# Attention scores of pooled keys: one product of 64 rows and 72 columns for each head in place of one of 128 rows and 144 columns for two

## The chip, the cores and the metric

The kernel runs on one core of a Trainium2 chip. The metric is the time of one execution on the device in microseconds (us); the median of three runs before is 1643.18 us (1641.29 to 1643.87).

## What is computed

Eight batches of eight heads, 576 queries, 576 keys and values of 64 numbers, all float32. Keys and values are first averaged over groups of 8, so each head has 72 pooled keys. Softmax attention over these 72 follows, and its output, 4608 rows of 512 numbers, goes through two two-layer networks.

```python
k_p = k.reshape(B, H, Sp, pool, D).mean(axis=3)      # B, H = 8, 8; Sp, pool, D = 72, 8, 64
v_p = v.reshape(B, H, Sp, pool, D).mean(axis=3)
scores = scale * np.matmul(q, k_p.transpose(0, 1, 3, 2))
scores = scores - np.max(scores, axis=-1, keepdims=True)
attn = np.exp(scores)
attn = attn / (np.sum(attn, axis=-1, keepdims=True) + 1e-09)
attn_out = np.matmul(attn, v_p)
...
h = x @ w_in;  x = np.maximum(0.01 * h, h) @ w_out   # first network, 512 -> 2048 -> 512
h = x @ w_in2; r = np.maximum(h, 0.0); out = (r * r) @ w_out2
```

## The kernel before

**Stages.** The attention is one generator, `attention()`. Its first batch is written out in order by hand (`first_batch`, L662); the other seven are advanced in pieces (`advance`, L1195) between the steps of the first network's first tiles, which TensorE works on in the same time (`first`, L851, and `second`, L881). All attention work is over at about 480 us. What follows, the rest of the first network and the whole second one, is products of 128 rows with 256 to 512 columns in TensorE's order, with none of the changed lines in it.

**The attention of a batch.** The 576 queries come in five chunks of 128, 128, 64, 128 and 128 tokens, named by their first token: 0, 128, 256, 320, 448. `prepare_k` (L422) pools the keys, transposes them (`trk`) and writes them into one of two tiles `kT` (L456 to L464); `prepare_v` does the values. For each chunk `stage_a` (L529) transposes the queries (`trq`), so that `qT[:, m]` holds the 64 numbers of head 2m on rows 0 to 63 and those of head 2m+1 on rows 64 to 127, for each of the `NP` = 4 pairs m. `stage_parts` (L545) makes the scores (L554), the negated maxima (L564), the exponentials (L571, or for the last three batches L576 and L580) and the normalised weights `p`; `keys_part` and `rest_part` (L599, L610) transpose these into `pt` and `pr`; `stage_d` (L629) multiplies with the values.

**The scores.** `kT` is a tile `[128, 4, 2, 72]`: of the 144 columns of a pair the first 72 hold the keys of head 2m on rows 0 to 63 with zeros below, the last 72 those of head 2m+1 on rows 64 to 127 with zeros above. The zeros are written once, at the start, by GpSimd (L347). So one product of all 128 rows, 144 columns wide, gives the scores of two heads side by side. Four such products make a chunk: two into the PSUM bank of score tile `s..._0` (heads 0 to 3), two into that of `s..._1` (heads 4 to 7). The queries are the weights that TensorE loads, 128 columns wide (64 in the 64-token chunk), and the keys stream.

**What sets the order.** The framework schedules the instructions of each engine from the code's order and its own costs when the kernel is built; each engine then runs its list strictly in that order, waiting where something isn't there. Score tiles come from a ring of four PSUM banks (`ps_w`; in the first batch `ps_a`), which the products `h` and `o` and the transposes use too.

Of the kernel before, what the change touches and what calls it, by code (L numbers as in the profile page):

```python
# [8 lines left out]
F32 = mybir.dt.float32  # L9
F32R = mybir.dt.float32r  # L10
U32 = mybir.dt.uint32
AF = mybir.ActivationFunctionType
ALU = mybir.AluOpType
# [4 lines left out]
P = 128  # L18
POOL = 8
KM = 64  # L20
# [7 lines left out]
def raw(ap):  # L28

    return ap.bitcast(F32)  # L30
# [3 lines left out]
def attention_two_mlps(  # L34
# [11 lines left out]
    nc = tc.nc  # L46
    B, H, S, D = q.shape
# [3 lines left out]
    SP = S // POOL  # L51
    KR = SP - KM
    NP = H // 2
# [82 lines left out]
    def work(name, n=TT, early=False):  # L136
        if early:
            return ps_a.tile([P, n], F32, tag="acc", name=name)
        return ps_w.tile([P, n], F32, tag="w", name=name)
# [182 lines left out]
    def attention():  # L322

        with ExitStack() as s:
# [4 lines left out]
            one = s.enter_context(tc.tile_pool(name="one", bufs=1, side="right"))  # L329
# [5 lines left out]
                out=mask, in_=mask, compare_op=ALU.is_ge, fill=0.0, base=0,  # L335
# [3 lines left out]
                out=mask, in_=mask, compare_op=ALU.is_ge, fill=0.0, base=KR - 1,  # L339
                pattern=[[KR, H], [0, D]], channel_multiplier=-1,  # L340
            )

            kT = [one.tile([P, NP, 2, SP], F32, name=f"kT{i}") for i in range(2)]
            vM = [one.tile([P, NP, 2, D], F32R, name=f"vM{j}") for j in range(2)]
            vR = one.tile([3 * RG, NP, 2 * D], F32R, name="vR")
            for i in range(2):
                nc.gpsimd.memset(kT[i], 0.0)  # L347
                nc.gpsimd.memset(raw(vM[i]), 0.0)
            pt_h = one.tile([P, NP, SPANS[0]], F32R, name="pt_h")
            pt_l = one.tile([P, NP, SPANS[0]], F32R, name="pt_l")  # L350
# [2 lines left out]
            def pooled(dst, src):  # L353

                for n in (POOL * D // 2, POOL * D // 4, D):
                    nc.vector.tensor_tensor(
                        out=dst if n == D else src[:, :, 0:n], in0=src[:, :, 0:n], in1=src[:, :, n:2 * n], op=ALU.add
                    )

            def pooled_pe(name, src):  # L360

                ps = work(name, NP * D).rearrange("p (m d) -> p m d", d=D)
                for m in range(0, NP, 2):
                    for j in range(POOL):
                        nc.tensor.matmul(
                            ps[:, m:m + 2], ident, src[m // 2][:, :, j * D:(j + 1) * D],
                            start=j == 0, stop=j == POOL - 1,
                        )
                    yield ps
# [52 lines left out]
            def prepare_k(b):  # L422
                kr, kk = KV.pop(("k", b))
                i = b % 2
                kd = ap1.tile([P, NP, D], F32, tag="kd", name=f"kd{b}")
                rr = ap1.tile([KR * H, 2, D], F32, tag="rr", name=f"rr{b}")
                pooled(rr[:, 0:1], kr)
                nc.vector.tensor_copy(rr[:, 1], rr[:, 0])
                if b in K_ON_PE:
                    for ps in pooled_pe(f"kp{b}", kk):  # L430
                        yield
                    nc.scalar.copy(kd, ps)
                else:
                    for m in range(0, NP, 2):
                        pooled(kd[:, m:m + 2], kk[m // 2])
                        if b > 0:
                            yield
                            continue
                        tr = work("trk0") if m == 0 else tr
                        nc.tensor.transpose(  # L440
                            tr[:, m * D:(m + 2) * D], kd[:, m:m + 2].rearrange("p a d -> p (a d)"), ident
                        )
                        yield
                if b > 0:
                    load_v(b)
                    tr = work(f"trk{b}")
                for g in range(2 if b > 0 else 0):
                    nc.tensor.transpose(
                        tr[:, g * P:(g + 1) * P], kd[:, 2 * g:2 * g + 2].rearrange("p a d -> p (a d)"), ident
                    )  # L450
                nc.tensor.transpose(
                    tr[:, 2 * P:2 * P + KR * H], rr.rearrange("p a d -> p (a d)"), ident[:KR * H, :KR * H]
                )
                for r in range(2):
                    rows = slice(r * D, (r + 1) * D)
                    nc.scalar.activation(  # L456
                        kT[i][rows, :, r, 0:KM], tr[rows, 0:2 * P].rearrange("p (m x) -> p m x", x=KM),
                        AF.Copy, scale=scale / POOL,
                    )
                    nc.scalar.activation(  # L460
                        kT[i][rows, :, r, KM:SP],
                        tr[rows, 2 * P:2 * P + KR * H].rearrange("p (m r x) -> p m r x", r=2, x=KR)[:, :, r],
                        AF.Copy, scale=scale / POOL,
                    )  # L464
                yield
# [48 lines left out]
            for b in range(B):  # L514
                at = 0
                for span in range(len(SPANS)):
                    off = 0
                    while off < SPANS[span]:
                        n = min(P, SPANS[span] - off)
# [21 lines left out]
            def stage_b(*chunk):  # L541
                for _ in stage_parts(*chunk):
                    pass

            def stage_parts(b, span, at, off, n):  # L545
                qT = qt.pop((b, at))
                x = xp.tile([P, H, SP], F32, tag="x", name=f"x{b}_{at}", bufs=2)
                sm, rs = (xp.tile([P, H, 1], F32, tag=g, name=f"{g}{b}_{at}") for g in ("sm", "rs"))
                scores = []
                for e in range(2):  # L550
                    sc = work(f"s{b}_{at}_{e}", early=b == 0)[:, :H // 2 * SP].rearrange("p (h x) -> p h x", x=SP)
                    scores.append(sc)
                    for m in range(2):
                        nc.tensor.matmul(  # L554
                            sc[:n, 2 * m:2 * m + 2].rearrange("p a x -> p (a x)"),
                            qT[:, 2 * e + m, :n],
                            kT[b % 2][:, 2 * e + m].rearrange("p a x -> p (a x)"),
                            start=True, stop=True,
                        )
                yield  # L560
                tops = []
                for e, sc in enumerate(scores):
                    mx = xp.tile([P, 4, 1], F32, tag="mx", name=f"mx{b}_{at}_{e}")
                    nc.vector.tensor_reduce(out=mx[:n], in_=sc[:n], axis=AX.X, op=ALU.max, negate=True)  # L564
                    tops.append(mx)
                yield
                for e, (sc, mx) in enumerate(zip(scores, tops)):
                    hs = slice(4 * e, 4 * e + 4)
                    if b < EARLY:
                        for h in range(4):  # L570
                            nc.scalar.activation(  # L571
                                x[:n, 4 * e + h], sc[:n, h], AF.Exp,
                                bias=mx[:n, h], accum_out=sm[:n, 4 * e + h],
                            )
                        continue
                    nc.vector.tensor_tensor(  # L576
                        out=x[:n, hs], in0=sc[:n], in1=mx[:n].to_broadcast([n, 4, SP]), op=ALU.add
                    )
                if b >= EARLY:
                    nc.scalar.activation(x[:n], x[:n], AF.Exp)  # L580
                    nc.vector.tensor_reduce(out=sm[:n], in_=x[:n], axis=AX.X, op=ALU.add)
                yield
                nc.vector.tensor_scalar(out=sm[:n], in0=sm[:n], scalar1=1e-9, scalar2=None, op0=ALU.add)
                nc.vector.reciprocal(rs[:n], sm[:n])
                pp = xp.tile([P, DM + 6 * RG], F32, tag="p", name=f"p{b}_{at}", bufs=2)
                nc.gpsimd.tensor_tensor(
                    out=pp[:n, 0:DM].rearrange("p (h x) -> p h x", x=KM), in0=x[:n, :, 0:KM],
                    in1=rs[:n].to_broadcast([n, H, KM]), op=ALU.mult,
                )
                for g in range(2):  # L590
                    hs = slice(4 * g, 4 * g + 4)
                    o = pp[:n, DM + 3 * g * RG:DM + 3 * (g + 1) * RG].rearrange("p (r h x) -> p r h x", r=3, x=KR)
                    nc.gpsimd.tensor_tensor(
                        out=o, in0=x[:n, hs, KM:].unsqueeze(1).to_broadcast([n, 3, 4, KR]),
                        in1=rs[:n, hs].unsqueeze(1).to_broadcast([n, 3, 4, KR]), op=ALU.mult,
                    )
                pr[b, at] = pp
# [199 lines left out]
            for i in range(nch + 1, len(chunks) + 1):  # L797
# [3 lines left out]
                if i < len(chunks):  # L801
                    b = chunks[i][0]
# [13 lines left out]

    ready, marks = [0], []
    att = attention()
    STORES, made = [], 0

# [485 lines left out]
```

## Time and profile before

| | |
|---|---|
| median of three runs | 1643.18 us |
| the profiled execution, its own time | 1641.07 us |
| its span, first to last instruction | 1639.3 us |
| TensorE (PE) busy | 1602.6 us, 98% |
| its weight loads (PEld) | 1466.8 us, 89% |
| VectorE (DVE) busy | 1388.1 us, 85% |
| ScalarE (ACT) busy | 1008.1 us, 61% |
| GpSimd (POOL) busy | 117.3 us, 7% |
| DMA queue of the data | 66.3% of 16 engines |
| mean granted clock of TensorE | 0.996 of 2.4 GHz |

Multiplies are recorded with the time in which their data passes the array and comes out; they overlap, so that the time one costs in a row of many is the distance between two starts, not the length of a record. Weight loads have records of their own (PEld) and lie beside the multiplies of the weights before. A float32 product that isn't a transpose is recorded as two multiplies with a load each; the kernel's products of 256 and more columns are in the one-multiply format (`F32R`). Of a form such as `128*64 128x144`, the first pair is rows and columns of the weights, the second what streams.

### The profile page before, as it was taken

To read this page: it belongs to the slowest core of one execution; us is meant where nothing else is said; L and a number is where in the kernel's file an instruction comes from. 1 tells how busy PE (TensorE), PEld (TensorE's weight loads), DVE (VectorE), ACT (ScalarE), POOL (GpSimd) and SP (SyncE) were. 2 spreads that over 40 slices of the span, in tenths; PEclk is the share of its full clock that TensorE was granted. 3 is DMA by queue.
4 is the path that set the end of the run, shared out by engine and by line. 5 is a ranking of instruction groups with operands and counts; after the bars stand their busy time and mean duration, and the time that the engine had idled before them with its cause. 6 is when DMAs were issued, how large, how long until landed. Compare 5 with 4: busy or idle time off the path is not lost.

```text
span 1639.3 us, 25990 instructions
## 1 busy us (share of the span) xinstructions
PE 1602.6 (98%) x9032; PEld 1466.8 (89%) x9032; DVE 1388.1 (85%) x2070; ACT 1008.1 (61%) x1930; POOL 117.3 (7%) x149
## 2 busy tenths in 40 slices
PE   5999999999999999999999999999999999999999
PEld 4877788888888999999999999998998998998997
DVE  6899776789889999979759589889789799799687
ACT  6777677755667867667557547456456455465454
POOL 4121222223110000000000000000000000000000
PEclk9999999999999999999999999999999999999999
DMA  8675554777547688887766764865865756756655
GB/s 212 190 203 169 144 134 139 233 217 224 180 157 257 244 284 296 265 304 231 225 190 204 236 186 151 281 196 149 275 187 176 254 177 198 241 171 209 196 167 167
DMA packets 223730, 340.94 MB, mean 208 GB/s; under 512 B 56176, under 2 KB 138096, under 8 KB 223600
## 3 DMA queue, kind: packets, MB, share of 16 engines
q1 hardware_dynamic: 223280, 338.76, 66.3%
q8 instruction: 72, 1.18, 0.3%
q10 hardware_dynamic: 320, 0.52, 0.1%
q14 instruction: 58, 0.48, 0.1%
HBM read 268.44 MB, written 69.21 MB: 206 GB/s over the span
## 4 chain that ended last, share of the span: by engine, by line
PE 83%; DVE 8%; ACT 4%; DMA 3%; issue 1%; SPq 0%; POOL 0%; ACTq 0%; DVEq 0%; POOLq 0%
PE psum L1078 14%; PE psum L317 14%; PE psum L319 14%; PE psum L318 14%; PE psum L1079 7%; PE h L317 3%; PE h L319 3%; PE h L318 3%; PE acc L318 3%; PE acc L319 2%; PE acc L317 2%; PE s L554 1%; ACT x L571 1%; DMA xs<-x 1%; DVE hl_out L245 1%
## 5 line engine op out<-in xcount | busy, mean ns | idle before, releaser
L1078 PE MATMUL psum<-wb_out,oh 128*128 128x512 f32 x1008 | 352.8, 394 | 0.0
L317 PE MATMUL psum<-xh,wb_in 128*128 128x384 f32 x1008 | 337.3, 335 | 2.2 <-ACT s L1052 1.2
L319 PE MATMUL psum<-xh,wb_in 128*128 128x384 f32 x1008 | 336.8, 334 | 0.0
L318 PE MATMUL psum<-xl,wb_in 128*128 128x384 f32 x1008 | 336.8, 334 | 0.0
L930 ACT CAST oh<-g 128x768 fp32r<-128x768 f32 x252 | 210.3, 836 | 160.1 <-PE psum L1078 89.3
L1079 PE MATMUL psum<-wb_out,ol 128*128 128x256 f32 x1008 | 281.8, 280 | 0.0
L931 DVE TENSOR_TENSOR ol<-g,oh 128x768 fp32r<-128x768 f32 x252 | 239.4, 954 | 17.4 <-ACT oh L930 14.9
L1078 PEld LDWEIGHTS psum<-wb_out,oh 128*128 128x128 f32 x1008 | 189.6, 188 | 43.1
L317 PEld LDWEIGHTS psum<-xh,wb_in 128*128 128x128 f32 x1008 | 189.2, 188 | 3.9 <-ACT s L1052 1.5
L318 PEld LDWEIGHTS psum<-xl,wb_in 128*128 128x128 f32 x1008 | 189.2, 188 | 0.2
L319 PEld LDWEIGHTS psum<-xh,wb_in 128*128 128x128 f32 x1008 | 189.2, 188 | 0.0
L1079 PEld LDWEIGHTS psum<-wb_out,ol 128*128 128x128 f32 x1008 | 188.8, 187 | 0.2
L984 ACT CAST wb_in<-wb_in 128x512 fp32r<-128x512 f32 x144 | 89.3, 621 | 146.4 <-DMA wb_in<-ws_in 141.4
L985 DVE TENSOR_TENSOR wb_in<-wb_in 128x512 fp32r<-128x512 f32 x144 | 98.7, 688 | 80.3 <-ACT wb_in L984 79.8
L934 DVE TENSOR_TENSOR g<-g,g 128x768 f32<-128x768 f32 x144 | 136.0, 952 | 1.5 <-ACT g L1006 1.0
L317 PE MATMUL h<-xh,hl_in 128*128 128x512 f32 (+1 forms) x320 | 121.8, 381 | 4.0 <-DVE pt_r L619 2.8
L317 PE MATMUL acc<-gh,hl_out 128*128 128x512 f32 (+1 forms) x320 | 120.2, 382 | 1.4 <-ACT hl_out L244 1.1
L318 PE MATMUL acc<-gl,hl_out 128*128 128x512 f32 (+1 forms) x320 | 118.6, 373 | 0.7 <-DVE gl L865 0.7
L319 PE MATMUL h<-xh,hl_in 128*128 128x512 f32 (+1 forms) x320 | 118.7, 371 | 0.0
L318 PE MATMUL h<-xl,hl_in 128*128 128x512 f32 (+1 forms) x320 | 118.1, 369 | 0.0
L319 PE MATMUL acc<-gh,hl_out 128*128 128x512 f32 (+1 forms) x320 | 117.9, 371 | 0.0
L318 PE MATMUL psum<-ol,wb_out 128*128 128x384 f32 x336 | 112.6, 335 | 0.0
(161 smaller groups left out, 3113.7 us busy)
## 6 DMA issues: line engine op xcount, KB each, us to landing
wb_in<-wd_in SPq DMA_DIRECT2D x108, 512.0 KB
wb_out<-wd_out SPq DMA_DIRECT2D x108, 512.0 KB
wb_in<-ws_in SPq DMA_DIRECT2D x144, 256.0 KB
wb_out<-ws_out SPq DMA_DIRECT2D x144, 256.0 KB
xs<-x SPq DMA_DIRECT2D x18, 768.0 KB
out_dram<-o SPq DMA_DIRECT2D x23, 384.0 KB
q<-in_q_dram SPq DMA_DIRECT2D x32, 256.0 KB
v<-in_v_dram SPq DMA_DIRECT2D x64, 128.0 KB
```

The lines of the kernel that those rows point to most:

```text
L245: nc.vector.tensor_tensor(out=lo, in0=w, in1=raw(hi), op=ALU.subtract)
L317: nc.tensor.matmul(outp, ah, bh, start=first, stop=False, **kw)
L318: nc.tensor.matmul(outp, ah, bl, start=False, stop=False, **kw)
L319: nc.tensor.matmul(outp, al, bh, start=False, stop=last, **kw)
L554: nc.tensor.matmul(sc[:n, 2 * m:2 * m + 2].rearrange("p a x -> p (a x)"), qT[:, 2 * e + m, :n], kT[b % 2][:, 2 * e + m].rearrange("p a x - ...
L930: nc.scalar.copy(hi, src)
L931: nc.vector.tensor_tensor(out=lo, in0=src, in1=raw(hi), op=ALU.subtract)
L934: nc.vector.tensor_tensor(out=out_, in0=a, in1=b, op=ALU.subtract)
L984: nc.scalar.copy(whole[:, 0], raw(whole[:, 1]))
L985: nc.vector.tensor_tensor(out=whole[:, 1], in0=raw(whole[:, 1]), in1=raw(whole[:, 0]), op=ALU.subtract)
L1078: nc.tensor.matmul(outp, ah, b, start=first, stop=False, skip_group_check=True)
L1079: nc.tensor.matmul(outp[:, 1], al, b[:, 0], start=False, stop=last, skip_group_check=True)
```

## The change

Each head gets a product of its own: the 64 rows of its queries and keys, 72 columns wide, 8 a chunk in place of 4. `kT` loses the dimension that held the zeros, and the two memsets of it go. The eight products alternate between the lower and the upper 64 rows, and the bank now goes by the half: the even heads (rows 0 to 63) go to score tile `s..._0`, the odd ones to `s..._1`. So the maxima, the exponentials and the sums of a tile are those of every other head, and L576 writes its result into every other block of 72 columns of `x`.

```diff
-            kT = [one.tile([P, NP, 2, SP], F32, name=f"kT{i}") for i in range(2)]
+            kT = [one.tile([P, NP, SP], F32, name=f"kT{i}") for i in range(2)]
...
-                nc.gpsimd.memset(kT[i], 0.0)
...
-                        kT[i][rows, :, r, 0:KM], tr[rows, 0:2 * P].rearrange("p (m x) -> p m x", x=KM),
+                        kT[i][rows, :, 0:KM], tr[rows, 0:2 * P].rearrange("p (m x) -> p m x", x=KM),
...
-                        kT[i][rows, :, r, KM:SP],
+                        kT[i][rows, :, KM:SP],
...
-                    for m in range(2):
-                        nc.tensor.matmul(
-                            sc[:n, 2 * m:2 * m + 2].rearrange("p a x -> p (a x)"),
-                            qT[:, 2 * e + m, :n],
-                            kT[b % 2][:, 2 * e + m].rearrange("p a x -> p (a x)"),
-                            start=True, stop=True,
-                        )
+                for m in range(NP):
+                    for r, sc in enumerate(scores):
+                        rows = slice(r * D, (r + 1) * D)
+                        nc.tensor.matmul(sc[:n, m], qT[rows, m, :n], kT[b % 2][rows, m], start=True, stop=True)
...
-                    hs = slice(4 * e, 4 * e + 4)
                     if b < EARLY:
-                        for h in range(4):
+                        for m in range(NP):
+                            h = 2 * m + e
                             nc.scalar.activation(
-                                x[:n, 4 * e + h], sc[:n, h], AF.Exp,
-                                bias=mx[:n, h], accum_out=sm[:n, 4 * e + h],
+                                x[:n, h], sc[:n, m], AF.Exp,
+                                bias=mx[:n, m], accum_out=sm[:n, h],
                             )
                         continue
                     nc.vector.tensor_tensor(
-                        out=x[:n, hs], in0=sc[:n], in1=mx[:n].to_broadcast([n, 4, SP]), op=ALU.add
+                        out=x[:n].rearrange("p (m r) x -> p r m x", r=2)[:, e], in0=sc[:n],
+                        in1=mx[:n].to_broadcast([n, NP, SP]), op=ALU.add,
                     )
```

The order that the framework makes of it differs on TensorE almost only in the score products. In the rows below `s_128_0` is the score tile 0 of chunk 128, `acc` and `h` are products of the first network, `trq` and `pt` transposes; the last pair of numbers is the output's shape. A typical group, chunk 128 of batch 2 on TensorE, stands before as

```order
L319 MATMUL acc_0_3_727<-gh_0_15_1753,hl_out_15_1760 128x512
L554 MATMUL s_128_0_1912<-kT_179,qT_128_1802 128x144 x2
L554 MATMUL s_128_1_1915<-kT_179,qT_128_1802 128x144 x2
L317 MATMUL h_1_1_1936<-xh_1_0_1831,hl_in_1_1866 128x512
L318 MATMUL h_1_1_1936<-xl_1_0_1832,hl_in_1_1866 128x512
```

and after the change (the score line is now L555) as

```order
L319 MATMUL acc_0_3_745<-gh_0_15_1791,hl_out_15_1798 128x512
L555 MATMUL s_128_0_1954<-kT_179,qT_128_1840 128x72
L555 MATMUL s_128_1_1955<-kT_179,qT_128_1840 128x72
L555 MATMUL s_128_0_1954<-kT_179,qT_128_1840 128x72
L555 MATMUL s_128_1_1955<-kT_179,qT_128_1840 128x72
L555 MATMUL s_128_0_1954<-kT_179,qT_128_1840 128x72
L555 MATMUL s_128_1_1955<-kT_179,qT_128_1840 128x72
L555 MATMUL s_128_0_1954<-kT_179,qT_128_1840 128x72
L555 MATMUL s_128_1_1955<-kT_179,qT_128_1840 128x72
L317 MATMUL h_1_1_1982<-xh_1_0_1873,hl_in_1_1908 128x512
```

Its neighbours, products of 128 rows, are the same; between them TensorE now changes to 64 rows and back. In six of the 40 groups the scheduler does not alternate the halves. Chunk 0 of batch 3 on TensorE stands before as

```order
L533 MATMUL trq_128_2397<-ident,q_128_2307 128x128 x4
L554 MATMUL s_0_0_2407<-kT_180,qT_0_2314 128x144 x2
L554 MATMUL s_0_1_2410<-kT_180,qT_0_2314 128x144 x2
L604 MATMUL pt_448_2431<-ident,p_448_2366 128x128 x4
L317 MATMUL h_1_6_2441<-xh_1_0_1831,hl_in_6_2337 128x512
```

and after the change (the transposes are now L532 and L601) as

```order
L532 MATMUL trq_128_2455<-ident,q_128_2361 128x128 x4
L555 MATMUL s_0_0_2465<-kT_180,qT_0_2368 128x72 x4
L555 MATMUL s_0_1_2466<-kT_180,qT_0_2368 128x72 x4
L601 MATMUL pt_448_2493<-ident,p_448_2424 128x128 x4
L317 MATMUL h_1_6_2503<-xh_1_0_1873,hl_in_6_2391 128x512
```

Here the four products of the lower rows come first and the four of the upper rows behind them. Of the six, three stand so (four and four), three as three, three, one and one.

## Rows read from the trace of the kernel before

**Rows 1.** Busy time by stretch: PE, PEld, DVE, ACT, POOL (instructions), clock, DMA.

```profile
core 0: us, PE busy (x) PEld busy (x) DVE busy (x) ACT busy (x) POOL busy (x), PEclk, DMA share, GB/s
...
10.00:45.00 35.00, 26.18 (x129) 20.98 (x128) 28.42 (x61) 26.35 (x117) 14.68 (x17) 0.85 0.76 201
...
60.00:185.00 125.00, 118.66 (x599) 95.93 (x598) 116.17 (x197) 97.49 (x258) 25.94 (x26) 1.00 0.63 185
185.00:400.00 215.00, 211.93 (x1143) 175.48 (x1142) 169.21 (x365) 142.66 (x445) 55.39 (x68) 1.00 0.62 180
400.00:480.00 80.00, 78.67 (x423) 65.10 (x423) 66.93 (x131) 49.09 (x102) 17.00 (x25) 1.00 0.52 161
...
640.00:900.00 260.00, 259.74 (x1498) 259.23 (x1497) 214.95 (x279) 169.24 (x241) 0.00 (x0) 1.00 0.74 237
```

**Rows 2.** The chain that ended last by line, 60 to 185, then 185 to 480.

```profile
by line: DVE wm L216 7.4%; DVE hl_out L245 5.8%; DVE w L226 5.7%; DVE gl L865 5.1%; issue 4.9%; ACT x L571 4.0%; DMA st_in_out<-in_moe_w_out_dram 3.5%; PE h L318 3.4%; DVE wm L209 3.4%; DVE mx L564 3.3%; PE h L317 3.3%; PE h L319 3.3%; DVE 
...
by line: PE h L317 10.0%; PE h L319 9.7%; PE h L318 9.7%; PE acc L317 8.9%; PE acc L319 8.7%; PE acc L318 8.6%; PE s L554 6.9%; ACT x L571 3.4%; PE trq L533 3.1%; PE pt L604 2.8%; PE o L638 2.1%; PE o L317 2.0%; PE o L318 2.0%; issue 1.9%; 
```

**Rows 3.** Groups by line and shape, the score products: busy us, mean ns, idle before.

```profile
L554 PE MATMUL s<-kT,qT 128*128 128x144 f32 x256 | 40.9, 304 | 1.6 <-DVE pt_l L606 0.9 <-ACT x L571 0.6
...
L554 PE MATMUL s<-kT,qT 128*64 128x144 f32 x64 | 10.6, 310 | 1.8 <-ACT qT L537 1.6 <-DVE pt_l L606 0.2
```

**Rows 4.** Timeline of PE, start us, length us, around one score group.

```profile
318.17 0.39 PE L319 MATMUL acc<-gh,hl_out 128*128 128x512 f32 x1
318.40 0.60 PE L533 MATMUL trq<-ident,q 128*128 128x128 f32 x4
318.83 1.15 PE L554 MATMUL s<-kT,qT 128*128 128x144 f32 x8
319.81 0.60 PE L604 MATMUL pt<-ident,p 128*128 128x128 f32 x4
```

**Rows 5.** Timeline of PE around transposes of 64 rows, from narrow windows.

```profile
244.52 0.29 PE L554 MATMUL s<-kT,qT 128*128 128x144 f32 x1
...
244.74 0.46 PE L604 MATMUL pt<-ident,p 64*128 64x64 f32 x4
245.04 0.27 PE L616 MATMUL pr<-ident,p 64*96 64x64 f32 x2
245.24 0.50 PE L317 MATMUL acc<-gh,hl_out 128*128 128x512 f32 x1
245.58 0.40 PE L318 MATMUL acc<-gl,hl_out 128*128 128x512 f32 x1
```

**Rows 6.** Timeline of PE and its loads (PEld) behind changes of rows, narrow windows.

```profile
225.37 0.39 PE L554 MATMUL s<-kT,qT 128*128 128x144 f32 x1
...
225.37 0.19 PEld L554 LDWEIGHTS s<-kT,qT 128*128 128x128 f32 x1
...
225.47 0.31 PEld L554 LDWEIGHTS s<-kT,qT 128*128 128x128 f32 x2
...
203.17 0.14 PEld L533 LDWEIGHTS trq<-ident,q 128*128 128x128 f32 x1
...
203.23 0.14 PEld L533 LDWEIGHTS trq<-ident,q 128*128 128x128 f32 x1
...
244.79 0.26 PEld L604 LDWEIGHTS pt<-ident,p 64*128 64x128 f32 x3
...
244.98 0.18 PEld L616 LDWEIGHTS pr<-ident,p 64*96 64x96 f32 x2
```

**Rows 7.** The score line L554: its loads, what it waited for, who waited.

```profile
L554 PEld LDWEIGHTS s<-kT,qT x320: 132/190/338, 12.6 to 464.6; 128*128 128x128 f32 x128, 128*64 128x64 f32 x32
...
  DVE pt_l L606: 3.0, 7
...
  DVE mx L564: 11.3, 15
```

**Rows 8.** A last memset of the first block on POOL; group of L576.

```profile
3.94 0.57 POOL L347 MEMSET kT<- 128x576 f32 x1
4.46 0.52 POOL L348 MEMSET vM<- 128x512 f32 x1
...
L576 DVE TENSOR_TENSOR x<-s,mx 128x288 f32<-128x288 f32 x24 | 9.8, 449 | 0.0
```

## The prediction

> **What bounds the kernel now.** I read first the busy time by stretch, then the chain that ended last in the same stretches, then TensorE's timeline instruction by instruction around one group of scores. The scores are made only in the first 480 us. From 185 to 400 us TensorE is busy 211.9 of 215 us and from 400 to 480 us 78.7 of 80, while VectorE stands at 169.2 and 66.9 [rows 1]; the chain from 185 to 480 us runs almost wholly over TensorE's lines, the score products L554 alone with 6.9% [rows 2]. So there a nanosecond added to TensorE is a nanosecond added to the end, and the stages behind, where TensorE is busy 259.7 of 260 us between 640 and 900 us, pass it on. From 60 to 185 us the chain is VectorE's decoding (L216, L245, L226) and TensorE has 6 us to spare [rows 1, 2]; from 10 to 45 us TensorE is busy 26.2 of 35 us. Ten of the 40 score groups (batches 0 and 1) lie before 185 us, thirty behind.
>
> **What a score group costs.** The group has four float32 products, each recorded as two multiplies, so eight: 318.83 to 319.81 us, 0.98 us, 0.122 us a step for 144 columns, that is 0.85 ns a column [rows 4]. The groups of 64 tokens (weights 64 columns wide) stream the same 144 columns [rows 3]. Over 40 groups this is 39.2 us. The load of the next weights hides under each multiply.
>
> **The loads.** This is where I expect the change to be paid for. When nothing covers it, a load of a score's 128 columns holds the engine for 0.10 to 0.11 us: loads at 225.37 and 225.47 [rows 6]. (The two records' lengths, 190 ns for 128 columns and 132 for 64, say the same: 0.058 us for 64 columns [rows 7].) Loads for transposes are twice as fast a column: 203.17 to 203.23, 0.06 us, on all 128 rows, and 0.063 us a step on 64 rows ((244.98 - 244.79) / 3) [rows 6]. Halving the rows did not halve that load; it goes by columns. The changed kernel loads as many columns as before for each product, has twice as many products, and only half as many columns to stream behind each: 72 columns are 0.061 us. A load of 0.107 no longer hides under 0.061.
>
> **The change, part by part.**
> (a) *Steady part of a group.* After the change 16 multiplies, each with its load. On one half of the rows a step is a load and the few ns that the next load starts behind the multiply, 0.11 us. The two multiplies of a product follow each other on the same half; if the other half loads and multiplies meanwhile, the second of one product runs beside the first of the next, which makes 8 steps and a last stream of 16 multiplies: 8 x 0.11 + 0.06 = 0.94 us against 0.98; 32 groups, -1.3 us. In the 8 groups of 64 tokens the load is half, the step 0.062, the group 0.56 us: 8 x -0.42 = -3.4 us. If the halves do not overlap: 15 x 0.11 + 0.06 = 1.71 us, +0.73 a group.
> (b) *Six groups whose halves the scheduler did not alternate* (one of them shown above with four and four): three with four and four have 15 steps in place of 8, three with three, three, one, one have 12: 3 x 0.77 + 3 x 0.44 = +3.6 us.
> (c) *Changing between 128 and 64 rows.* The trace has this already, for the transposes of 64-token chunks. Going in: from the last score multiply at 244.52 to the first of the `pr` transposes at 245.04 are 0.52 us, where 0.122 + 4 x 0.063 = 0.37 would do: 0.15, of which 0.10 before the first instruction (244.74) and 0.05 for its uncovered load. Going out: 245.04 to 245.58 are 0.54 us against two steps of 0.06 and one of 0.23 (318.17 to 318.40): 0.19, say 0.20, the uncovered load now being 0.107 [rows 4 to 6]. In the program's order TensorE changes 50 times before and 112 times after: 31 more pairs, not 40, since a group beside `trq`, `pt` or `pr` of 64 rows shares their change. A score group going in pays 0.20 (0.15 for 64 columns), going out 0.20, or 0.15 where transposes follow; a pair lies between 0.30 and 0.40, I take 0.37: +11.5 us.
> (d) *Both banks at once.* The first two products now need both PSUM banks of a group, where the second was needed half a group later, and both maxima (L564) wait for the end of the group. L554 sat waiting for a bank's reader 7 times, 3.0 us (the loads' waits included), L564 for L554 15 times, 11.3 us [rows 7]. Half a group more on some of these is 0 to 2 us on TensorE; VectorE has 46 us of slack between 185 and 400 us, which hides its part. I take 0.8 us.
> (e) *Priced at nothing.* The two memsets of the keys (0.57 us each) go, but the last memset of that block ends at 4.98 us [rows 8] and the keys' first product is at 12.6 [rows 7]. The strided write of L576 is the same 288 elements; if its 24 full-size instructions of 449 ns [rows 8] grew by half, 5 us would fall on VectorE's slack behind 300 us. Fewer exponentials or copies there are not.
>
> Sum on TensorE: -1.3 - 3.4 + 3.6 + 11.5 = +10.4 us. Three quarters lie behind 185 us and count in full, of the first quarter I count half: 7.8 + 1.3, and 0.8 from (d): **+10 us**. The profiled execution took 1641.07 us, the median of three runs 2.1 us more. 1651 by the one, **1653 us** by the other.
>
> A rule of the Trainium skill weighed here (TensorEngine Tiling (Array Packing), Overview, Theoretical Speedup): a contraction of at most 64 rows is said to allow up to twice the speed. By it the 39.2 us would become 19.6 and the kernel some 1624 us; by the rows it is +10, because the loads and the changes of rows are not in that rule. No run here shows two halves at work at once.
>
> **Rivals.**
> *B, the forecast: the halves overlap, loads included.* For it: after a change of rows the multiply is recorded at 225.37, together with its own load [rows 6]; so the engine takes in a multiply whose weights are not there yet, and can take the next load behind it. Against it: all 64-row work of the trace lies on the lower rows, so two loads at once appear nowhere. 1653, with a pair in (c) between 0.30 and 0.40 and (d) between 0 and 2: 1650 to 1655.
> The same page (Tiling Modes, Key Properties) states that different tiles can load and multiply in parallel; by it B, without it C; no row decides.
> *C, the change does not do what it says: loads follow one another.* Then all 16 loads stand in a row: 32 x 0.73 + 8 x 0.01 + 11.5 = +35 us, with half of the first quarter off +31: 1674; with the first quarter free 1669, in full 1678. For it: where loads are seen one by one they follow each other, 225.37 and 225.47 on the same rows [rows 6], and never lie two deep.
> *Between:* some of the loads overlap, about 1660.
> *D, faster: loads of half the rows are quick.* If a load of 64 rows takes 0.055, or runs ahead, every group is 8 x 0.062 + 0.06 = 0.56 us: 40 x -0.42 = -17, (b) +2, changes 31 x 0.31 = +9.6: -5 us, 1638. It decides from a load of 0.06 or less. Against it: the transposes' load, equal on 64 and 128 rows.
> *No change:* (c) half as dear in a stream where both neighbours are quick, or TensorE's extra time falling into its idle 4.4 us behind 185 us: within 3.3 us.
>
> **How the numbers follow.** B 0.50, C 0.25, between 0.05, D 0.12, no change 0.08. B is twice C because the row of the early multiply speaks for taking in loads ahead; D is low because the load rows speak against it. Faster 0.12, same 0.08, slower 0.80, by 0.2% or 3.3 us, about what a measurement of this kernel can tell from no change. The range 1645 to 1678 leaves out D (0.12), most of no change and the upper edge of C (0.08 together).
>
> **What would show it.** In the profile after: TensorE's score records double to 640, with a load each. (a) right: a group of 128 tokens lasts 0.9 to 1.0 us from its first full-speed multiply to its last, in pairs 0.11 apart; C right: 16 even steps of 0.11, 1.7 us; D right: steps of 0.03 or pairs of 0.06. (c) right: 0.2 us between the product before a group and the group, and again behind it. TensorE's busy time and idle gaps from 185 to 480 us must carry the whole difference, and the stage from 640 us on must keep its length. The forecast is wrong if the load of 64 rows differs from 0.107, or if changing rows costs nothing when the other half is the one that follows.

## The result, and the profile after

The changed kernel takes 1650.68 us in the median of five runs (1649.17 to 1652.74), the kernel before beside it 1641.29 us (1639.47 to 1643.87, five runs): ratio 1.0056, 95% interval 1.004 to 1.0071, so 9.4 us slower. The profiled execution took 1651.65 us, its span is 1649.9 us.

First the same stretches as in [rows 1] (columns as there).

```profile
PE 1613.1 (98%) x9352; PEld 1472.8 (89%) x9352; DVE 1386.0 (84%) x2070; ACT 1007.8 (61%) x1930; POOL 115.9 (7%) x147
...
60.00:185.00 125.00, 119.42 (x635) 96.52 (x634) 112.96 (x187) 95.91 (x250) 26.66 (x26) 0.97 0.60 180
185.00:400.00 215.00, 212.35 (x1293) 173.91 (x1291) 168.05 (x364) 141.04 (x447) 54.00 (x69) 1.00 0.62 179
400.00:480.00 80.00, 77.47 (x478) 63.23 (x479) 65.41 (x131) 48.17 (x99) 16.79 (x25) 1.00 0.52 160
640.00:900.00 260.00, 256.60 (x1475) 255.26 (x1475) 212.47 (x276) 171.28 (x242) 0.00 (x0) 1.00 0.74 239
```

TensorE's busy time grew by 10.5 us (1602.6 before), but it isn't fuller from 400 to 480 us (77.47 for 78.67), and the stage from 640 us on, which the prediction wanted unchanged, has 3.4 us of gaps for 0.3. Of these, 1.4 us are a wait at 644 us that the kernel before has at 635 us (1.2 us), ahead of this window; from 640 us to the end the changed kernel takes 1.2 us longer in this execution and 0.1 in a second one. The granted clock from 60 to 185 us is 0.97, not 1.00.

Next the group of scores that stood for all. The first fence is TensorE's timeline (start us, length us) of the usual group and a group of 64 tokens with their neighbours, and the loads and multiplies in windows that end a few ns apart, so that the count shows what began between two window ends (371.378 and 371.383; 371.545 and 371.55; 371.658 and 371.67).

```profile
371.06 0.39 PE L319 MATMUL acc<-gh,hl_out 128*128 128x512 f32 x1
371.38 1.11 PE L555 MATMUL s<-kT,qT 64*128 64x72 f32 x16
372.42 0.66 PE L601 MATMUL pt<-ident,p 128*128 128x128 f32 x4
...
240.47 0.60 PE L532 MATMUL trq<-ident,q 128*128 128x128 f32 x4
241.00 0.72 PE L555 MATMUL s<-kT,qT 64*64 64x72 f32 x16
241.65 0.66 PE L601 MATMUL pt<-ident,p 128*128 128x128 f32 x4
...
371.37 0.18 PEld L555 LDWEIGHTS s<-kT,qT 64*128 64x128 f32 x1 [0.35 <-issue]
...
371.37 0.19 PEld L555 LDWEIGHTS s<-kT,qT 64*128 64x128 f32 x2 [0.35 <-issue]
...
371.38 0.44 PE L555 MATMUL s<-kT,qT 64*128 64x72 f32 x3
...
371.38 0.45 PE L555 MATMUL s<-kT,qT 64*128 64x72 f32 x4
...
371.38 0.55 PE L555 MATMUL s<-kT,qT 64*128 64x72 f32 x5
...
371.38 0.56 PE L555 MATMUL s<-kT,qT 64*128 64x72 f32 x6
```

Two loads begin 0.007 us apart, one on each half of the rows, and so do the multiplies: third and fourth at 371.542 and 371.549, fifth and sixth at 371.654 and 371.661, and so on to 372.212 and 372.219. (A record doesn't name its half. That a pair is a lower and an upper product follows from the kernel below with four lower products first, where the first steps come singly.) The trace agrees here with the Trainium skill (TensorEngine Tiling (Array Packing), Tiling Modes, Key Properties: different tiles load and multiply in parallel). A pair comes each 0.112 us, a load of 128 columns. From the first multiply's start to the last's are 0.843 us; before, 0.856 to 0.860. The speedup of up to 2 that the Trainium skill gives (TensorEngine Tiling (Array Packing), Overview, Theoretical Speedup) does not come in this group: 0.843 for 0.860.

The group of 64 tokens does gain: its pairs are 0.062 us apart, 0.495 us from first to last where it was 0.909. But its weights are 64 columns wide, and the *kernel before* already paid for a change of form there, which I had overlooked. Its timeline:

```profile
288.35 0.39 PE L319 MATMUL h<-xh,hl_in 128*128 128x512 f32 x1
288.67 1.20 PE L554 MATMUL s<-kT,qT 128*64 128x144 f32 x8
289.80 0.44 PE L604 MATMUL pt<-ident,p 128*128 128x128 f32 x2
...
66.13 0.39 PE L317 MATMUL acc<-gh,hl_out 128*128 128x512 f32 x1
66.36 0.65 PE L554 MATMUL s<-kT,qT 128*128 128x144 f32 x4
```

From the product to the first score are 0.32 us at 288.35, all 128 rows but 64 columns; 0.23 us at 66.13, where nothing of the form changes. After the change the usual group has the 0.32 too (371.06 to 371.38).

Last the score line's waits (idle us, times), to be read beside [rows 7].

```profile
L555 PEld LDWEIGHTS s<-kT,qT x640: 129/188/335, 12.4 to 472.8; 64*128 64x128 f32 x128, 64*64 64x64 f32 x32
...
  DVE pt_l L603: 6.4, 10
...
  DVE mx L560: 14.2, 13
```

The waits for a bank's last reader, VectorE's `pt_l`, went from 3.0 to 6.4 us. The largest is new:

```profile
399.16 0.39 PE L319 MATMUL h<-xh,hl_in 128*128 128x512 f32 x1
399.48 0.34 PE L555 MATMUL s<-kT,qT 64*64 64x72 f32 x2
401.56 0.71 PE L555 MATMUL s<-kT,qT 64*64 64x72 f32 x14 [1.74 <-DVE pt_l L603]
...
92.76 0.71 PE L555 MATMUL s<-kT,qT 64*64 64x72 f32 x14 [0.16 <-DVE pt_l L603]
96.24 0.47 PE L317 MATMUL h<-xh,hl_in 128*128 128x512 f32 x1 [2.77 <-DVE pt_r L616]
...
97.98 0.63 PE L317 MATMUL h<-xh,hl_in 128*128 128x512 f32 x1
98.41 0.63 PE L318 MATMUL h<-xl,hl_in 128*128 128x512 f32 x1
...
397.80 1.53 DVE L862 TENSOR_TENSOR gl<-g,gh 128x512 fp32r<-128x512 f32 x1
...
400.22 0.68 DVE L245 TENSOR_TENSOR hl_out<-w,hl_out 128x512 fp32r<-128x512 f32 x1
400.83 0.68 DVE L603 TENSOR_TENSOR pt_l<-pt,pt_h 128x512 fp32r<-128x512 f32 x1
```

At 399.48 the first head's two multiplies run; the next head's need the other bank, which `pt_l` still has to read. VectorE works without a gap and comes to it at 400.83. And behind 96.24 us, where TensorE had waited 2.77 us, products soon come 0.43 us apart instead of 0.23: the granted clock is 0.5 (1.2 GHz) from 97.4 us for 3.4 us. The kernel before waited as long at the same place and kept its full clock (there TensorE had no idle time in the 4 us ahead of the wait; here it had 0.57 and 0.16 us):

```profile
88.77 1.24 PE L554 MATMUL s<-kT,qT 128*64 128x144 f32 x8
92.79 0.47 PE L317 MATMUL h<-xh,hl_in 128*128 128x512 f32 x1 [2.77 <-DVE pt_r L619]
93.10 0.39 PE L318 MATMUL h<-xl,hl_in 128*128 128x512 f32 x1
...
93.78 0.39 PE L318 MATMUL h<-xl,hl_in 128*128 128x512 f32 x1
...
393.85 1.20 PE L554 MATMUL s<-kT,qT 128*64 128x144 f32 x8
...
393.30 0.68 DVE L606 TENSOR_TENSOR pt_l<-pt,pt_h 128x512 fp32r<-128x512 f32 x1
```

The last two rows answer the wait at 399 us: the same `pt_l` began 0.55 us ahead of the group here, and half a group's time was left before the second bank was needed.

### The profile page after: what moved, and what is told of

It is laid out like the page before. It is cut to its first block, busy times and chain, and to the rows that moved or that the text cites. A ratio compares the mean times of both kernels' runs of the same rounds, so it can differ in the third digit from the quotient of the medians.

```text
span 1649.9 us, 26631 instructions
## 1 busy us (share of the span) xinstructions
PE 1613.1 (98%) x9352; PEld 1472.8 (89%) x9352; DVE 1386.0 (84%) x2070; ACT 1007.8 (61%) x1930; POOL 115.9 (7%) x147
## 4 chain that ended last, share of the span: by engine, by line
PE 79%; DVE 9%; ACT 5%; DMA 4%; issue 2%; POOL 0%; SPq 0%; DVEq 0%; ACTq 0%; POOLq 0%
PE psum L1075 14%; PE psum L317 13%; PE psum L319 13%; PE psum L318 13%; PE psum L1076 7%; PE h L317 2%; PE acc L318 2%; PE h L318 2%; PE h L319 2%; PE acc L319 2%; PE acc L317 2%; ACT x L567 2%; PE s L555 2%; DMA st_in_out<-in_moe_w_out_dram 1%; DVE hl_out L245 1%
```

## Where the time comes in

ScalarE computes `g` from `h` (L861 before, L858 after) at the same places of the program in every kernel here; the delay of some of them against the kernel before (profiled execution against profiled execution) shows where time is lost. "Again" are further executions of the two kernels unchanged; the other columns belong to the experiments below.

| at (us, before) | before again | after | after again | banks | late | early | only 64 | late 64 |
|---|---|---|---|---|---|---|---|---|
| 47 | -0.3 | +1.7 | -0.1 | +0.7 | 0.0 | +2.3 | +1.1 | -0.7 |
| 88 | -0.4 | +3.5 | +1.5 | +0.2 | +0.2 | +4.1 | +0.9 | -1.1 |
| 200 | -0.2 | +6.0 | +4.4 | +0.5 | +2.8 | +5.4 | +3.7 | 0.0 |
| 362 | -0.2 | +5.4 | +4.9 | -0.2 | +3.1 | +5.4 | +4.2 | +0.3 |
| 403 | -0.2 | +7.4 | +8.5 | +1.6 | +5.0 | +5.4 | +3.9 | +0.1 |
| 484 | -0.6 | +9.2 | +9.9 | +1.2 | +5.9 | +5.9 | +4.2 | -0.5 |
| span's end | -0.7 | +10.6 | +9.4 | +1.7 | +8.0 | +5.1 | +5.0 | +1.3 |

The forecast had 1.3 us up to 185 us, and an even rise of 8.6 behind. The trace has 4 to 6 us up to 200, nothing from 200 to 362, 2.0 to 3.6 between 362 and 403, 1.4 to 1.8 more until 484; behind that, where no line was changed, +1.4 in one execution and -0.5 in the other.

What TensorE itself loses between 200 and 484 us I took from the distances between starts, leaving out distances that a wait lengthened: nothing between the two executions of the kernel before, +1.7 us after. A count that enters each lengthened distance at its usual length gives +2.2 to +2.6, and puts the early kernel below, whose scores in this stretch are those of before, 0.7 to 0.9 us up; such sums are good to about 1 us. Group by group it reads: 13 usual groups cost 0.15 to 0.25 us more each from the product before to what follows, the five beside 64-row transposes 0.03 less except for one un-alternated (+0.42), the groups of 64 tokens 0.476 less.

## Experiments

**The banks alone.** The kernel before, with its pairs of heads alternating between the two banks: all but the halves.

```diff
-                    for m in range(2):
-                        nc.tensor.matmul(
-                            sc[:n, 2 * m:2 * m + 2].rearrange("p a x -> p (a x)"),
-                            qT[:, 2 * e + m, :n],
...
+                for m in range(NP):
+                    nc.tensor.matmul(
+                        scores[m % 2][:n, m // 2 * 2:m // 2 * 2 + 2].rearrange("p a x -> p (a x)"),
+                        qT[:, m, :n],
```

> The products of the kernel before (128 rows, 144 columns, zero blocks), but the four pairs of heads go to the two score banks in turn, so that both banks are needed from the second product on and complete only at the end of a group. No product of 64 rows. If the extra time of the changed kernel is TensorE's (changes between 128 and 64 rows), this is the time of the kernel before, at most 1 us more. If it comes from needing both banks early and from the order that the scheduler then makes, a good part of the 9.4 us appears here: 3 to 7 us more, with waits of the score line for a bank's reader (L606) well above the 3.0 us of before.

1643.08 us against 1642.24, ratio 1.0001 [0.9991, 1.001]: nothing. A wait of 1.5 us for `pt_l` appeared at 394 us here too (+1.6 at 403 us in the table), so that wait belongs to the banks, not to the halves, and yet the median doesn't show it. This kernel also has a stretch of half clock at 92.9 us, 3.4 us long, without a loss in the median.

**Late and early.** The changed products in batches 2 to 7 alone, or in batches 0 and 1 alone; elsewhere the kernel before.

```diff
+            def halves(b, n):
+                return b > 1
...
+                for m in range(NP if halves(b, n) else 0):
+                    for r, sc in enumerate(scores):
+                        rows = slice(r * D, (r + 1) * D)
+                        nc.tensor.matmul(sc[:n, m], qT[rows, m, :n], kT[b % 2][rows, m, r], start=True, stop=True)
```

> The changed products in batches 2 to 7 only, the old ones in batches 0 and 1; zero blocks stay in the keys. By the prediction's sum three quarters of the cost are here: 8 us more than before. By the spacings in the trace of the changed kernel TensorE loses 0.26 us in a group of 128 tokens, gains 0.48 in one of 64 and is even where transposes of 64 rows stand beside it: some 0.25 us a batch, 1.5 us in all, and with 1 to 2.5 us of waits for banks 2.5 to 4 us more than before.

> The changed products in batches 0 and 1 only, the old ones behind. By the prediction 1.3 to 2.6 us more than before. By the trace of the changed kernel, which is 5.5 us late at 186 us, 4 to 6 us more, from waits behind a changed order on VectorE and ScalarE, since TensorE's own extra in these ten groups is under 3 us.

Late: 1648.92 us against 1642.24, 1.0037 [1.0023, 1.005], +6.7. Early: 1644.01, 1.0008 [0.9999, 1.0016], +1.8. Together 8.5 of 9.4. So by the medians three quarters of the loss do come from the late groups. The early kernel's profiled execution took 1646.22 us, 2.2 over its median, so its column in the table overstates the first quarter; the row at 47 us alone differs by 1.8 us between the two executions of the changed kernel. Late gives TensorE +1.3 to +1.8 us of its own from 200 to 484 us; the rest of the 8.0 us of its profiled execution are the start (+2.8 at 200 us), idle time (4.9 us for 3.8 between 200 and 484 us, the same 1.7 us wait among it, here up to 399 us) and 2.1 us behind 484 us. Two stretches of half clock, 3.4 us each, lie in there, both where TensorE sets the time. The second follows a wait of 1.9 us:

```profile
711.94 0.45 PE L317 MATMUL psum<-xh,wb_in 128*128 128x384 f32 x1 [1.87 <-ACT s L1058]
...
713.27 0.52 PE L317 MATMUL psum<-xh,wb_in 128*128 128x384 f32 x1
713.59 0.52 PE L318 MATMUL psum<-xl,wb_in 128*128 128x384 f32 x1
```

For ten steps products come 0.32 us apart in place of 0.174, about 1.5 us. From 190.6 us seven steps are 0.43 us in place of 0.23, about 1.4 us, and in the 8 us before that TensorE had idled only 0.32 and 0.31 us. So some 3 of the 8 us of this execution are half clock. The medians carry no such share: over all executions the mean granted clock is 0.9939 here (eight), 0.9944 in the changed kernel (five) and 0.9946 in the kernel before (46); in that kernel 0.001 less goes with about 0.7 us more. By that estimate half clock makes 0.5 us or less of the difference between the medians.

**The 64-token groups alone.** Line as above, with `n < P`: the eight groups that save TensorE most.

> The changed products only in the eight groups of 64 tokens. By the prediction (-0.42 us of streaming, two changes of rows 0.30 to 0.35) the same as before within 1 us. By the trace of the changed kernel these groups already changed the tile form in the kernel before (0.318 us in, 0.216 out), so that the change is a pure gain of 0.48 us each: 3.8 us less than before on TensorE, 2 to 4 us less in time if no wait takes it.

1644.46 us, 1.0009 [1.0, 1.0018]: no gain, where the expectation had one. TensorE's own time from 200 to 484 us fell by 1.3 to 1.7 us, its idle time rose by 1.1 (4.9 for 3.8), and stretches of half clock (6.8 us from 93.0, 3.4 us from 140.7) stand where 88 to 200 us lost 2.8.

**The same two kernels again.** To see what of one profile repeats.

> The kernel before, unchanged, profiled once more. If the half-clock stretches and the waits behind 590 us differ from the first profile by chance, this one has other ones, and the pieces of the difference that rest on them (3.4 us of half clock at 97 and 142 us, 2.5 us behind 590 us) are scatter; if they repeat, each costs what the pair of traces shows.

> The changed kernel, unchanged, profiled once more. Scatter: the half-clock stretches at 97 and 142 us lie elsewhere or are gone and the landmarks behind them move by 1.5 us each; the wait of 1.9 us inside the score group at 399.6 us follows from the order of the instructions and is there again in either theory.

1640.39 and 1650.49 us. The half-clock stretches repeat to within 3 us: before at 20 and 37 us in both, after at 37 to 39, 95 to 97 and 140 to 142. Only the second execution of the changed kernel has one at 402.4 us, behind the wait at 399 us, and there TensorE's own time is 1.4 us more: 3.4 us at half clock cost it 1.4 us, as in the late kernel. At the start the clock is first recorded as full at 32.5 us in one execution of the changed kernel and at 27.0 in the other (16 to 17 us in the kernel before), which goes with the 1.8 us between the two at 47 us.

**Four lower products, then four upper.**

```diff
-                for m in range(NP):
-                    for r, sc in enumerate(scores):
+                for r, sc in enumerate(scores):
+                    for m in range(NP):
                         rows = slice(r * D, (r + 1) * D)
```

> The changed kernel with the four products of the lower rows ahead of the four of the upper rows in every group, so that the halves hardly overlap. If loads and multiplies of the two halves run at the same time in the changed kernel, a group of 128 tokens now takes 15 steps of 0.11 us in place of 7 or 8, 0.7 to 0.8 us more in the 34 groups that alternated (those of 64 tokens 0.4): 15 to 24 us more than the changed kernel, about 1668. If alternation gave nothing, the same 1651.

1658.88 us in one run, 8.4 above the changed kernel beside it (1650.49): slower, as expected, but half as much. One group's multiplies, and what had begun by 275.98 and 275.99 us:

```profile
275.48 1.62 PE L555 MATMUL s<-kT,qT 64*128 64x72 f32 x16
277.03 0.50 PE L317 MATMUL acc<-gh,hl_out 128*128 128x512 f32 x1
...
275.76 0.38 PE L555 MATMUL s<-kT,qT 64*128 64x72 f32 x2
...
275.76 0.56 PE L555 MATMUL s<-kT,qT 64*128 64x72 f32 x4
```

The group lasts 1.344 us from first start to last, 12 steps of 0.112 us, not 15. At 275.987, between the two window ends, a load of the upper half begins beside the lower half's fifth multiply, 0.51 us after the group began and with three lower multiplies still to come. So the halves overlap somewhat even in this order. It also gives the size of step (b): +0.50 us a group, not 0.77. And TensorE's idle time from 200 to 484 us fell to 1.2 us from 4.2 in the changed kernel: part of what was added went into its waits.

**The zeros kept, 72 columns each.** All 128 rows and 72 columns for each head: as many columns loaded and streamed as in the changed kernel, no halves.

```diff
+                        nc.tensor.matmul(sc[:n, m], qT[:, m, :n], kT[b % 2][:, m, r], start=True, stop=True)
```

> The zero blocks stay and all products have 128 rows, but each head is its own product of 72 columns, alternating between the banks as in the changed kernel: no change of rows, no overlap of halves. If a load of 128 columns (0.107 us) can't hide under 72 columns of streaming (0.061), each of the 16 multiplies takes 0.11 us and a group 1.75 us in place of 0.98: 32 x 0.77 = 24 us more than the kernel before. If a load were as quick as the streaming, the same as before.

```profile
252.15 0.39 PE L319 MATMUL acc<-gh,hl_out 128*128 128x512 f32 x1
252.38 1.90 PE L566 MATMUL s<-kT,qT 128*128 128x72 f32 x16
```

1662.43 us in one run, 19.4 over the kernel before. From first to last are 1.62 us in fifteen steps, the first of 0.062 us and the others of 0.112: a load of 128 columns stands in each of these, and the 72 columns streamed hide beneath it. This is what the changed kernel would have been without the overlap, its changes of rows aside; entering the group costs 0.23 us here (252.15 to 252.38), so it is the halves that make it 0.32.

**Work in the wait.** The changed kernel, with the scores of one chunk made five times, so that TensorE has something to do at 91 to 94 us.

```diff
-                for m in range(NP):
+                for m in list(range(NP)) * (5 if (b, at) == (1, 256) else 1):
```

> The changed kernel, but the scores of one chunk (256 of batch 1) are made five times over the same bank before they are read; the values are the same. TensorE then works through the 2.9 us in which it waited at 91 to 94 us of the changed kernel (h, line 317, for DVE's pt_r), on whose heels its granted clock fell to 0.5 for 3.4 us in both traces of the changed kernel. Theory 'the half-clock stretch is part of the price': four more groups cost at most 4 x 0.85 = 3.4 us of TensorE there, of which the wait of 2.9 us hides most; the stretch at 95 to 98 us is gone, worth 1.38 us by the other one that was priced, so the kernel comes out 0.5 to 1.4 us under the changed kernel's 1650.7, some 1649.3 to 1650.2, ratio to the kernel before about 1.0047. Rival 'the stretch hides behind other engines': the stretch is gone and the time the same or up to 0.5 us more, 1650.7 to 1651.2. Rival 'the stretch has nothing to do with the wait': it stays at 95 to 98 us although TensorE didn't wait.

1654.66 us, 1.0072 [1.0058, 1.0086]: none of the three. The scheduler ordered what follows differently; TensorE waited a little later, and the half clock came behind that:

```profile
102.87 0.39 PE L613 MATMUL pr<-ident,p 128*96 128x128 f32 x2 [1.84 <-DVE mx L560]
105.06 0.68 PE L317 MATMUL h<-xh,hl_in 128*128 128x512 f32 x1 [1.79 <-ACT x L567]
105.54 0.63 PE L318 MATMUL h<-xl,hl_in 128*128 128x512 f32 x1
```

The stretch followed the wait to its new place, from 97.4 to 105.2 us; that speaks for a tie between the two, and against a fixed place. The late kernel's stretch at 190.6 us shows that one can also come without a long wait. What such a stretch costs in the first quarter this run doesn't say, as the order changed too (+8.3 us at 124 us).

**The late 64-token groups alone.** With `b > 1 and n < P`: the part of the change that saves TensorE time, in the stage that TensorE sets.

> The changed products only in the six groups of 64 tokens of batches 2 to 7, the kernel before everywhere else. Those groups changed the tile's form in the kernel before already, so each saves TensorE 0.476 us and adds no change of form: 6 x 0.476 = 2.9 us. Nothing differs from the kernel before up to 185 us, so neither do the stretches of half clock there. Theory 'the loss of the kernel with all eight 64-token groups changed came from the first quarter': 1639.5 to 1642, at or under the kernel before, ratio 0.998 to 1.000. Rival 'the gain turns into waits wherever it is made, for ScalarE's and VectorE's pt halves and the second bank': the wait at 399 us grows by up to 1.9 us and others appear of 0.3 to 0.9 us, and the time is 1641.5 to 1644, ratio 1.000 to 1.001.

1643.0 us against 1642.54, 1.001 [1.0001, 1.0018]: the rival, and no version better than the kernel before. At 200 us nothing differs (0.0; the -1.1 at 88 us, where the scores are made as before, is scatter), and no half clock is added. From there to 484 us TensorE's own time is 1.6 to 2.7 us less, by the way it is counted, and its idle time 1.2 us more (5.0 for 3.8). The largest new wait is at 248 us; TensorE and ScalarE there in this kernel, and ScalarE in the kernel before:

```profile
247.45 0.39 PE L319 MATMUL acc<-gh,hl_out 128*128 128x512 f32 x1
248.55 0.41 PE L317 MATMUL o<-pt_h,vM 128*128 128x320 f32 x1 [0.71 <-ACT pt_h L615]
...
245.71 0.32 ACT L581 ACTIVATE x<-s,mx 128x72 f32<-128x72 f32 x1 [1.68 <-DVE mx L571]
...
248.10 0.40 ACT L615 CAST pt_h<-pt 128x256 fp32r<-128x256 f32 x1
```

```profile
245.23 0.37 ACT L605 CAST pt_h<-pt 128x256 fp32r<-128x256 f32 x1 [0.75 <-PE pt L604]
245.68 0.32 ACT L571 ACTIVATE x<-s,mx 128x72 f32<-128x72 f32 x1
```

Before, ScalarE copies `pt_h` as soon as `pt` is there and makes the eight exponentials after it. The list that the framework builds for this kernel has the exponentials first; ScalarE then sits 1.68 us until their maxima are there, and `pt_h` comes 2.9 us later, with `o` of TensorE behind it. So the largest of these waits comes not from a unit at its limit, but from another order of ScalarE's list. At 344 us 0.47 us go into a wait for VectorE's `x`. Of 0.476 us saved five times, 0.5 are left at 484 us, and behind that, where no line was changed, this execution loses 1.8 us more.

## Why the prediction was right or wrong

The time, its sign, and the likeliest case were right: +9.4 us against +10, and B is what the trace shows. The sum that led there was not: it had 6 to 7 us too much on TensorE and left out about 6 that arose elsewhere. That the two cancelled to within 1 us was luck.

*What bounds the kernel.* Right for TensorE's own steps; wrong in taking TensorE as free of waits. "A nanosecond added to TensorE is a nanosecond added to the end" does not hold as it stands: part of what is added goes into the waits that are there (idle time of 1.2 us for 4.2 in the kernel with four lower products first), and what is saved went into new ones (the two runs with 64-token groups), the largest of them shown to come from a changed order on ScalarE.

*The loads.* Right. A load goes by columns (0.107 to 0.112 us for 128, 0.062 for 64, on 64 rows and on 128), and 72 streamed columns don't cover it: the zeros-kept kernel. Case C would have been that kernel's step of 0.112 plus the changes of rows; D is excluded by the pairs at 0.112.

*(a).* Right in size, with another picture. I had the two multiplies of one product beside those of the next, staggered, 8 steps. They run as lower beside upper, 7 steps of 0.112 us, 0.784 for 0.860: -0.076 a group, -2.4 for 32, not -1.3. (The 0.843 measured has the first load uncovered, 0.166 us for the first step; that is counted in (c).) The 64-token groups: -0.476 each with their changes, not -0.42, -3.8 for eight.

*(b).* Predicted +3.6, found about +2.5: 1.1 for the three pieces of batch 1's first two groups (63.76, 68.68 and 72.66 us; the last two 0.84 us for 0.37 and 0.42), 0.2 to 0.5 each for four behind 185 us. The steps were counted too high: four and four take 12, not 15. Two groups of the first batch (22.38 and 27.83 us) are 0.25 to 0.7 us longer than before as well, but they alternate; their steps are 0.213 us in place of 0.112, and in the second execution, with full clock from 27.0 us on, the later one lasts 0.837 us.

*(c).* This is the term that failed, by its count more than by its price. 31 pairs at 0.37 us made +11.5. Eight of the 31 were the 64-token groups, which changed the form already: 23 are left. A pair costs 0.09 us ahead of the first load (0.32 for 0.23; 0.20 for 0.11 behind `trq`), 0.05 for that load uncovered, where I had 0.10, and 0.17 going out into a product (0.20 for 0.03) or 0.13 into `pt` (0.20 for 0.12, and its first step 0.164 for 0.109), where I had 0.20 and 0.15. The 13 usual groups behind 200 us give 0.29 on average, so 23 x 0.29 = 6.7.

With these the sum on TensorE is -2.4 - 3.8 + 2.5 + 6.7 = +3.0, not +10.4; between 200 and 484 us the trace has 1.7 to 2.6 of it.

*(d).* Price about right, mechanism half: the banks alone measured a ratio of 1.0001, no difference, and TensorE's idle time between 200 and 484 us grew by 0.5 us (4.2 for 3.8), by 1.3 in the second execution, where 0.8 was priced. In the late stage a 1.9 us wait for the second bank stood at 399 us, partly paid for by one for GpSimd's `p` at 212 us that went (1.4). The reading [rows 7] showed the waits by sum; where the next one would fall can't be read from it.

*Not in the sum at all:* the first quarter, where 4 to 6 us arise in the profiles and 1.8 in the early kernel's median, for the 1.3 counted; what differs behind 484 us, +1.4 us in one execution and -0.5 in the other, where TensorE waits 0.5 to 1.9 us for ScalarE's `s` at places that vary from execution to execution, in the kernel before too (1.2 and 1.1 us at 635 us, 0.6 at 704 in one); and stretches of half clock, 1.4 to 1.5 us each in the three that could be priced, which weigh in single profiles but, by the mean clocks, hardly in the medians.

*(e).* Nothing contradicts it: VectorE's busy time fell by 2 us as a whole.

**Open.** TensorE's own 1.7 to 2.6 us behind 200 us, 0.5 to 1.3 us of idle time there and the first quarter's 1.8 us in the median leave some 4 to 5 of the 9.4 us without a shown cause. Why the 2.77 us wait at 90 us is followed by half clock in the changed kernel and not in the kernel before, and what such a stretch costs there: the banks run had one and lost nothing, the 64-token run lost about 2 us where it had one of twice the length, and the attempt to fill the wait moved it. Of the late part's 6.7 us in the median, 1.3 to 1.8 are TensorE's own and about 1 is idle time up to 484 us; the half clock of its profiled execution is not in the median, and the rest wasn't settled. Taking the scheduler's order out of it, by a kernel in which only the products change and every other engine's list stays word for word, wasn't tried.

## What to carry to other kernels

Halving the rows of a product pays only where the load of its weights hides: compare columns loaded with columns streamed first (128 loaded for 72 streamed: 0.843 us for 0.860; 64 for 72: 0.495 for 0.909). Price the change of form per neighbour, from a row where it stands alone, and count which products already pay it. A saving on the busiest engine is worth what the next wait leaves of it: look at the lists of the other engines as built, since a shorter group can reorder them. And before half clock seen in one profile is taken for the price of a change, compare the mean granted clock of all executions of both kernels.

## What the runs showed of the hardware

- Two halves of the rows load and multiply at the same time, 0.007 us apart, each half at its own pace of one load a step (0.112 us for 128 columns).
- Weights of 64 columns on all 128 rows change the form as much as 64 rows do: 0.32 us in for 0.23, 0.216 out into `pt` for 0.122.
- A load for the other half begins although three multiplies of the first half, earlier in the program, still have to start (275.99 us in the kernel with four lower products first). So between the halves TensorE doesn't begin its list strictly in order, as the section on the kernel before has it of every engine.
- The granted clock fell to half for 3.4 us behind waits of 1.7 to 2.8 us, but not behind each of them: two waits of 2.77 us at the same place of two kernels, one followed by 0.43 us a product, the other by 0.23. Once it fell with no idle time over 0.32 us in the 8 us before (the late kernel, 190.6 us).
